# Layer-norm shift terms on GpSimd, a normalisation on ScalarE, and a reordered start in a two-block transformer kernel

## The chip, the core and the metric

The kernel runs on one core of a Trainium2 chip. The core has five engines with queues of their own: TensorE (PE in the profile; PEld is its weight load), VectorE (DVE), ScalarE (ACT), GpSimd (POOL) and SyncE (SP), which here only issues DMAs. The metric is the device time of one execution in microseconds (us), the median of several runs.

## The reference, cut to what matters

The sequence has S = 2048 rows of D = 448; H = 16 heads of 28; Fh = 896.

```
mod = silu(c) @ w_mod                 # sa, ca, ga, sb, cb, gb, each 448
h = layernorm(x) * (1 + ca) + sa
q, k, v = h @ wqkv
phi_q = [softmax(q @ w_phi), softmax(-(q @ w_phi))]   # phi_k likewise
o = (phi_q @ (phi_k.T @ v)) / (phi_q @ sum(phi_k) + 1e-6)   # linear attention
x = x + ga * (o @ wo)
h = layernorm(x) * (1 + cb) + sb
z = gelu(h @ w_in);  z1 = z[:, :Fh];  z2 = layernorm(z[:, Fh:])
g = w_sp @ z2 + b_sp                  # w_sp is 2048 x 2048
x = x + gb * ((z1 * g) @ w_out)
```

## The kernel before, in words

The program is `fast_path`, written with a manual schedule: each engine executes its instructions in the order in which the Python code emits them, and a general path for large weights exists that this input doesn't take. There are NT = 16 tiles of 128 rows. Products accumulate in PSUM, in four single banks (`bank`) and two double banks (`bank2`).

**Setup (lines 541 to 709).** First loads go out on the queues of SP and ScalarE. `silu(c)` is made as a column (`scol`); `colform` multiplies it by slices of w_mod and gives a modulation vector as a column. Scale and shift of the layer norm are folded into the weights: `fold_T` transposes raw k weights on TensorE, `fold_pf` multiplies them by the block-diagonal matrix `BD` of w_phi and by 1 + ca (`ca1`), `fold_sa` and `bias_row` make the bias rows. `l1_stats`, `l1_rstd` and `l1_apply` normalise a tile of x: VectorE takes mean and variance (L603, L604), GpSimd adds epsilon (L608) and raises to the power -0.5 (L609), VectorE forms the shift term `nmr` = -mean * rstd (L611), and the tile is scaled and shifted (L616) and transposed by a DMA on SP (L618).

**Stage 1 (lines 847 to 894)** loops over the tiles: products with Wv and Wk (`k_mm`), two exponentials on ScalarE, the softmax normalisation on VectorE (`k_norm`), accumulation of phi_k.T @ v (`kv_acc`). In the same loop q's weights are folded (`late`), q's products and exponentials are made for four tiles at once (`q_mm`, `q_exp`), and the loads of all later weights are issued (`loads`, `load_wsp`). SP takes its DMAs in order, so that a load stands behind the transposes emitted ahead of it. At the end `KVbd` is built from the accumulator, and `norm_sq` and `norm_max` test the weights' norms for the flag that chooses the path.

**Stage 2 (lines 998 to 1021)** is a software pipeline over j = 0 to 23. Iteration j works on eight different tiles:

```
l2_apply(j-4)   # L608, L609 GpSimd; L611 nmr VectorE; L616 GpSimd; DMA transpose to h2T
num_fin(j-1)    # L917 Sx ScalarE; L919-L926 cr .. t VectorE; L928 GpSimd; DMA to oT
z2_norm(j-7)    # L983 VectorE
wo_mm(j-3)      # L937, L939 TensorE; L940 ScalarE
z2_stats, z2_rstd(j-6)   # L969, L971 VectorE; L977, L978 GpSimd
l2_stats(j-3)   # L603, L604 VectorE
z2_mm(j-5)      # L960 TensorE; L963 Gelu ScalarE
z1(st, fc)      # L990 TensorE, L991 Gelu ScalarE: j 9 to 20, two of 7 chunks (one each 4th j)
num_mm(j)       # L909 TensorE
```

At j = 21 the last seven z1 units run. The order within an iteration is the order on each engine's queue.

**Stage 3 (lines 1031 to 1068)** multiplies w_sp by z2 in 28 groups of 16 matmuls (`g_unit`, L1035), adds b_sp, multiplies by z1, and makes the output product (L1042).

## Time and profile before

| what | value |
|---|---|
| median of 3 runs | 318.06 us (318.04 to 318.09) |
| profiled execution, its own time | 317.58 us |
| its span, first to last instruction | 315.7 us |
| TensorE busy | 266.4 us (84%) |
| VectorE busy | 179.2 us (57%) |
| ScalarE busy | 94.1 us (30%) |
| GpSimd busy | 92.1 us (29%) |

The profiled execution's own time is 1.9 us longer than its span. Busy shares are means over stages with different limits. The first product of stage 1 starts at 20.70 us, the first of stage 2 at 87.72 us, the first of stage 3 at 190.12 us.

### The profile page before, as it was taken

The page shows a single profiled execution, that of the slowest core. Times are in us where ns is not written, and L with a number is a line of the kernel's source. Part 1 is how long each engine was busy: PE and PEld are TensorE (multiplying, and loading weights), DVE is VectorE, ACT ScalarE, POOL GpSimd, SP SyncE. Part 2 cuts the span into 40 slices and gives each one's busy share as a digit, 9 for nine tenths or more (in the row PEclk, how much of TensorE's full clock was granted, in tenths as well). Part 3 has the DMA queues.
Part 4 walks back from the last instruction along what each step waited for, and adds up shares of the span by engine and source line. Part 5 has one row for each costly group of instructions (what it writes and reads, how often), then busy time and mean ns, then how long its engine had stood idle before and what let it go on. Part 6 is the DMA issues. An engine that isn't in the chain of part 4 may idle for free. (4 is left out here: it accounts for less than half of the span.)

```text
span 315.7 us, 4217 instructions
## 1 busy us (share of the span) xinstructions
PE 266.4 (84%) x1500; PEld 132.0 (42%) x1524; DVE 179.2 (57%) x395; ACT 94.1 (30%) x179; POOL 92.1 (29%) x174
## 2 busy tenths in 40 slices
...
GB/s 184 121 144 122 204 227 243 110 103 166 49 17 50 68 53 33 50 52 39 47 52 51 33 203 173 208 220 2 15 29 15 2 29 28 4 16 15 31 0 65
DMA packets 71038, 25.81 MB, mean 82 GB/s; under 512 B 60960, under 2 KB 70880, under 8 KB 71008
## 3 DMA queue, kind: packets, MB, share of 16 engines
...
## 5 line engine op out<-in xcount | busy, mean ns | idle before, releaser
L1035 PE MATMUL g_ps<-f_wsp,f_z2n 128*128 128x512 bf16 x437 | 97.7, 379 | 0.5
L1035 PEld LDWEIGHTS <-f_z2n 128*128 128x128 bf16 x448 | 43.9, 98 | 52.2
L1037 DVE TENSOR_TENSOR gb<-g_ps,f_bsp 128x512 f32<-128x512 f32 x28 | 19.4, 692 | 69.4 <-PE g_ps L1035 67.4
L960 PE MATMUL z_ps<-f_win,h2T 128*128 128x448 bf16 (+1 forms) x128 | 27.1, 354 | 13.6 <-DMA h2T<-f_xpad 13.6
L990 PE MATMUL z_ps<-h2T,f_win 128*128 128x512 bf16 (+1 forms) x106 | 25.6, 379 | 0.3
L928 POOL TENSOR_TENSOR f_opad<-t 128x448 bf16<-128x448 bf16 x16 | 18.4, 1151 | 23.8 <-DVE t L926 19.3
L616 POOL TENSOR_SCALAR f_xpad<-f_x,rstd,nmr 128x448 bf16<-128x448 bf16 x30 | 22.6, 757 | 8.9 <-DVE nmr L611 3.1
L1042 PE MATMUL o_ps<-f_wout,f_z1T 128*128 128x448 bf16 x112 | 23.6, 352 | 1.8 <-DVE ot L1046 1.8
L963 ACT ACTIVATE z2g<-z_ps 128x896 bf16<-128x896 f32 x16 | 14.7, 917 | 30.7 <-PE z_ps L960 26.6
L960 PEld LDWEIGHTS <-h2T 128*128 128x128 bf16 (+1 forms) x128 | 11.2, 97 | 27.1 <-DMA h2T<-f_xpad 17.8
L939 PE MATMUL x_ps<-f_wo,oT 128*128 128x448 bf16 x64 | 17.9, 381 | 3.1 <-DMA oT<-f_opad 3.1
L1038 DVE TENSOR_TENSOR f_z1T<-gb,f_z1T 128x512 bf16<-128x512 f32 x28 | 19.4, 692 | 1.9 <-DVE gb L1037 0.5
L759 ACT ACTIVATE f_Eq<-q_ps 112x1024 bf16<-112x1024 f32 x16 | 16.2, 1024 | 13.2 <-PE q_ps L753 13.1
L753 PE MATMUL q_ps<-f_hT,f_Wq 128*128 128x512 bf16 (+1 forms) x57 | 14.8, 379 | 4.8 <-DVE f_Wq L663 2.4
L731 DVE TENSOR_REDUCE sums<-f_E 128x32 f32<-128x896 bf16 x16 | 17.2, 1072 | 2.4 <-ACT f_E L726 2.4
L969 DVE BATCH_NORM_STATS2 stats<-z2g 128x6 f32<-128x448 bf16 x32 | 18.3, 615 | 0.1
L991 ACT ACTIVATE f_z1T<-z_ps 128x512 bf16<-128x512 f32 x28 | 16.7, 597 | 4.3 <-PE z_ps L990 4.3
L926 DVE TENSOR_TENSOR t<-num,w 128x896 bf16<-128x896 f32 x16 | 17.5, 1091 | 0.6
L720 PE MATMUL v_ps<-f_Wv,f_hT 128*128 128x448 bf16 x64 | 16.2, 379 | 1.0 <-DMA f_hT<-f_xpad 0.9
L990 PEld LDWEIGHTS <-f_win 128*128 128x128 bf16 x112 | 10.9, 97 | 12.8
L1042 PEld LDWEIGHTS <-f_z1T 128*128 128x128 bf16 x112 | 11.0, 98 | 11.8 <-issue 1.0
L909 PE MATMUL num<-f_KVbd,f_Eq 112*128 112x120 bf16 x128 | 10.0, 226 | 6.9 <-ACT z2g L963 3.0
...
## 6 DMA issues: line engine op xcount, KB each, us to landing
...
```

Source lines behind the costliest of these rows:

```text
L616: eng.tensor_scalar(out=xp[:, 0:D], in0=x_sb[:, i, :], scalar1=rstd[:, t:t + 1], scalar2=nmr[:, t:t + 1], op0=ALU.mult, op1=ALU.add)
L731: nc.vector.tensor_reduce(out=sums[:], in_=E[:].rearrange("p s (c f h) -> p (s c) h f", c=4, h=HP), axis=AX.X, op=ALU.add)
L926: nc.vector.tensor_tensor(out=t[:], in0=nv[:, :, :, 0:DH], in1=w[:].unsqueeze(3).to_broadcast([P, 2, H, DH]), op=ALU.mult)
L928: nc.gpsimd.tensor_tensor(out=op_[:, 0:D], in0=t[:, 0].rearrange("p h d -> p (h d)"), in1=t[:, 1].rearrange("p h d -> p (h d)"), op=ALU.add)
L939: nc.tensor.matmul(x1[:, 0:D], lhsT=oT[0:KD[cc], cc, :], rhs=wo_s[0:KD[cc], cc, :], start=False, stop=(cc == KC - 1))
L960: nc.tensor.matmul(z_ps[:, hf, 0:D], lhsT=h2[0:KB[kc], kc, il * P:(il + 1) * P], rhs=win_s[0:KB[kc], kc, FH + hf * D:FH + (hf + 1) * D], s ...
L969: nc.vector.bn_stats(out=stats[:, hf, :], in_=z2gs[i][:, hf, :])
L990: nc.tensor.matmul(z_ps[:], lhsT=win_s[0:KB[kc], kc, fc * P:(fc + 1) * P], rhs=h2[0:KB[kc], kc, :], start=(kc == 0), stop=(kc == KC - 1))
L1035: nc.tensor.matmul(g[:], lhsT=z2n[:, s_, fc * P:(fc + 1) * P], rhs=wsp_tiles[tcn][:, s_, :], start=(s_ == 0), stop=(s_ == NT - 1))
L1037: nc.vector.tensor_tensor(out=gb[:], in0=g[:], in1=bsp[:, tsl], op=ALU.add)
L1038: nc.vector.tensor_tensor(out=z1T[:, fc, tsl], in0=gb[:], in1=z1T[:, fc, tsl], op=ALU.mult)
L1042: nc.tensor.matmul(o_ps, lhsT=z1T[:, fc, t * P:(t + 1) * P], rhs=wout_s[:, fc, :], start=(fc == 0), stop=(fc == FC - 1))
```

## The change

The shift term of a layer norm (`nmr`) is computed by GpSimd, one instruction a tile, in place of VectorE. z2 is normalised by ScalarE (Identity with a scale and a bias operand), a few calls later in the iteration, and its shift term is made by GpSimd. In setup the k weights come on SP's queue, c comes as a row and is transposed by TensorE, `BD` is made by GpSimd, 1 + ca is made before the fold, `fold_T` alternates ScalarE and VectorE for k too, and weight slices and pads are widened to 128 columns. In stage 1 k's product comes ahead of v's; the late steps move two iterations forward; squares of the weights (`norm_sq`) are spread over iterations 4 to 11; the scaling of `win_s` goes from VectorE (iterations 14 and 15) to GpSimd (12 to 15); wsp0's transposes go from iterations 10 to 13 to 13 to 15 and after; w_out's load goes from iteration 6 to the start of stage 2, b_sp's from iteration 7 to the end of stage 2. The last q product is made in two halves in single banks, with the norm products between, ahead of kv_acc(15).

```diff
-    wk_raw = aph.tile([P, KC, D], BF, name="f_wk_raw")
+    wk_raw = aph.tile([P, KC, D + 16], BF, name="f_wk_raw")
...
-        nc.sync.dma_start(out=cT[:], in_=c.rearrange("o (k p) -> p (o k)", p=DC))
+    nc.sync.dma_start(out=c_row[:], in_=c)
     nc.scalar.dma_start(out=wm1[:, :, D:960], in_=wmod_v[:, :, D:960])
     nc.sync.dma_start(out=x_sb[:, 0:2, :], in_=xv[:, 0:2, :])
-    load_rows(nc.scalar, wk_raw[:], A_wqkv[:, D:2 * D])
-    nc.sync.dma_start(out=x_sb[:, 2:4, :], in_=xv[:, 2:4, :])
     nc.scalar.dma_start(out=wm1[:, :, 0:D], in_=wmod_v[:, :, 0:D])
+    load_rows(nc.sync, wk_raw[:, :, 0:D], A_wqkv[:, D:2 * D])
...
+    nc.sync.dma_start(out=x_sb[:, 2:4, :], in_=xv[:, 2:4, :])
     load_rows(nc.sync, Wv[:], A_wqkv[:, 2 * D:3 * D])
...
-        nc.vector.scalar_tensor_tensor(out=nmr[:, 0:n], in0=mv[:, 0:n, 0], scalar=-1.0, in1=rstd[:, 0:n], op0=ALU.mult, op1=ALU.mult)
+        for t in range(n):
+            nc.gpsimd.tensor_scalar(out=nmr[:, t:t + 1], in0=mv[:, t, 0:1], scalar1=rstd[:, t:t + 1], scalar2=-1.0,
+                                    op0=ALU.mult, op1=ALU.mult)
...
-    fold_T(wk_raw, wTk, False)
     l1_rstd(0)
-    l1_apply(0, nc.vector)
-    l1_apply(1, nc.vector)
-    l1_stats(2)
-    l1_stats(3)
-    nc.vector.tensor_tensor(out=BD[:].rearrange("p g (f h) -> p g f h", h=HP),
+    nc.gpsimd.tensor_tensor(out=BD[:].rearrange("p g (f h) -> p g f h", h=HP),
...
     one_plus(colform(wm1, 1), ca1)
+    l1_apply(0, nc.vector)
+    l1_apply(1, nc.vector)
+    fold_T(wk_raw, wTk)
     for m in range(3):
-        fold_pf(wTk, Wk, m, 0)
+        fold_pf(wTk, Wk, m, m % 2)
+    l1_stats(2)
+    l1_stats(3)
+    l1_rstd(1)
     cf = colform(wm1, 0)
     nc.vector.tensor_copy(out=sapad[:, :, 64], in_=cf[:, 0:4])
-    l1_rstd(1)
+    fold_sa(wk_raw, wTk)
     bv = bias_row(sapad, Wv, 0, D)
-    fold_sa(wk_raw, wTk)
+    fold_pf(wTk, Wk, 3, 0)
...
-        elif i == 5:
+        elif i == 13:
             nc.sync.dma_start(out=wmg[:, :, D:2 * D], in_=wmod_v[:, :, 5 * D:6 * D])
-        elif i == 6:
-            nc.sync.dma_start(out=wout_s[:], in_=B_w_out.rearrange("(k p) n -> p k n", p=P))
-        elif i == 7:
-            nc.sync.dma_start(out=bsp[:], in_=B_b_sp.partition_broadcast(P))
...
+        if 4 <= i < 12:
+            norm_sq((i - 4) // 4, (i - 4) % 4)
+        if i >= 12:
+            kk = i - 12
+            nc.gpsimd.tensor_scalar(out=win_s[0:KD[kk], kk, :], in0=win_s[0:KD[kk], kk, :], scalar1=cb1[0:KD[kk], kk:kk + 1],
+                                    scalar2=0.0, op0=ALU.mult, op1=ALU.add)
...
-        if 10 <= i < 14:
-            load_wsp(0, i - 10)
-        if i == 13:
-            norm_sq(0)
+        if i >= 13:
+            load_wsp(0, i - 13)
+    load_wsp(0, 3)
...
+    for u in range(2):
+        q1 = bank("q1_ps")
+        cc = 2 + u
+        for kc in range(KC):
+            nc.tensor.matmul(q1[:], lhsT=Wq[0:KB[kc], kc, cc * CB:cc * CB + P], rhs=hT[0:KB[kc], kc, 3 * 512:4 * 512],
+                             start=(kc == 0), stop=(kc == KC - 1))
+        n_pss.append(norm_mm(u))
+        for s in range(2):
+            nc.scalar.activation(out=Eq[0:CB, cc, s, 3 * 512:4 * 512], in_=q1[0:CB, :], func=ACT.Exp, scale=1.0 - 2.0 * s)
     kv_acc(NT - 1)
...
-    norm_max(0)
-    norm_sq(1)
-    q_mm(7)
-    q_exp(7, 0)
-    q_exp(7, 1)
-    norm_max(1)
+    for u in range(2):
+        nc.vector.tensor_reduce(out=mx[:, u:u + 1], in_=n_pss[u][0:1, 0:D], axis=AX.X, op=ALU.max)
...
-        z2mv[i] = (mv, rstd)
+        nmr = sm.tile([P, 1], F32, tag="z2nm")
+        nc.gpsimd.tensor_scalar(out=nmr[:], in0=mv[:, 0, 0:1], scalar1=rstd[:], scalar2=-1.0, op0=ALU.mult, op1=ALU.mult)
+        z2mv[i] = (nmr, rstd)
...
-        nc.vector.tensor_scalar(out=z2n[:, i, :], in0=z2gs.pop(i)[:].rearrange("p a d -> p (a d)"), scalar1=mv[:, 0, 0:1], scalar2=rstd[:],
-                                op0=ALU.subtract, op1=ALU.mult)
+        nc.scalar.activation(out=z2n[:, i, :], in_=z2gs.pop(i)[:].rearrange("p a d -> p (a d)"), func=ACT.Identity, scale=rstd[:],
+                             bias=nmr[:])
...
+    nc.sync.dma_start(out=wout_s[:], in_=B_w_out.rearrange("(k p) n -> p k n", p=P))
     for j in range(NT + 8):
...
-        if on(j - 7):
-            z2_norm(j - 7)
         if on(j - 3):
             wo_mm(j - 3)
...
             l2_stats(j - 3)
+        if on(j - 7):
+            z2_norm(j - 7)
         if on(j - 5):
             z2_mm(j - 5)
...
+    nc.sync.dma_start(out=bsp[:], in_=B_b_sp.partition_broadcast(P))
```

## Rows read from the trace of the kernel before

**Rows 1.** Stretches: length, busy time and instructions of each engine, PEclk, DMA share, GB/s.
```profile
20.70:87.70 67.00, 60.52 (x428) 32.95 (x433) 51.10 (x103) 43.62 (x74) 23.07 (x33) 1.00 0.70 157
...
119.30:171.60 52.30, 41.62 (x236) 19.76 (x239) 40.47 (x107) 22.89 (x49) 31.73 (x55) 1.00 0.24 46
171.60:190.10 18.50, 16.44 (x77) 7.20 (x77) 10.84 (x26) 10.16 (x16) 10.71 (x21) 1.00 0.57 111
190.10:307.60 117.50, 116.92 (x547) 54.52 (x557) 45.16 (x68) 0.60 (x1) 3.73 (x4) 1.00 0.25 52
```

**Rows 2.** Timeline of VectorE, 128 to 139 us: start, duration, instruction, idle before.
```profile
130.19 0.19 DVE L919 TENSOR_TENSOR cr<-num,Sx 128x32 f32<-128x32 f32 x1
...
132.26 0.50 DVE L983 TENSOR_SCALAR f_z2n<-z2g,z2mv,rstd 128x896 bf16<-128x896 bf16 x1
...
135.90 0.16 DVE L611 SCALAR_TENSOR_TENSOR nmr<-l2mv,rstd 128x1 f32<-128x1 f32 x1 [1.12 <-POOL rstd L609]
```

**Rows 3.** Timeline of TensorE, 128 to 139 us.
```profile
133.59 1.69 PE L960 MATMUL z_ps<-f_win,h2T 128*128 128x448 bf16 x8 [0.86 <-DMA h2T<-f_xpad]
135.12 1.90 PE L990 MATMUL z_ps<-h2T,f_win 128*128 128x512 bf16 x7
136.86 0.58 PE L909 MATMUL num<-f_KVbd,f_Eq 112*128 112x120 bf16 x8
```

**Rows 4.** Timeline of TensorE, 106 to 115 us.
```profile
109.73 0.58 PE L909 MATMUL num<-f_KVbd,f_Eq 112*128 112x120 bf16 x8 [0.97 <-ACT z2g L963]
110.14 0.35 PE L937 MATMUL x_ps<-f_x,f_ident 128*128 128x448 bf16 x1
...
111.29 1.69 PE L960 MATMUL z_ps<-f_win,h2T 128*128 128x448 bf16 x8
113.99 0.58 PE L909 MATMUL num<-f_KVbd,f_Eq 112*128 112x120 bf16 x8 [1.01 <-ACT z2g L963]
```

**Rows 5.** Timeline of GpSimd, 128 to 139 us.
```profile
132.43 1.23 POOL L928 TENSOR_TENSOR f_opad<-t 128x448 bf16<-128x448 bf16 x1 [1.25 <-DVE t L926]
134.16 0.22 POOL L977 TENSOR_SCALAR rstd<-z2mv 128x1 f32<-128x1 f32 x1 [0.51 <-DVE z2mv L971]
...
135.01 0.22 POOL L608 TENSOR_SCALAR rstd<-l2mv 128x1 f32<-128x1 f32 x1
...
136.23 0.75 POOL L616 TENSOR_SCALAR f_xpad<-f_x,rstd,nmr 128x448 bf16<-128x448 bf16 x1 [0.36 <-ACT z2g L963]
```

**Rows 6.** Timeline of GpSimd, 106 to 115 us.
```profile
109.67 1.03 POOL L928 TENSOR_TENSOR f_opad<-t 128x448 bf16<-128x448 bf16 x1 [1.25 <-DVE t L926]
```

**Rows 7.** Groups of ScalarE by line and shape: count, busy us, mean ns, idle.
```profile
L991 ACT ACTIVATE f_z1T<-z_ps 128x512 bf16<-128x512 f32 x28 | 16.7, 597 | 4.3 <-PE z_ps L990 4.3
...
L963 ACT ACTIVATE z2g<-z_ps 128x896 bf16<-128x896 f32 x16 | 14.7, 917 | 30.7 <-PE z_ps L960 26.6 <-DVE stats L969 4.1
...
L940 ACT CAST f_x<-x_ps 128x448 bf16<-128x448 f32 x16 | 8.5, 532 | 16.3 <-PE x_ps L939 16.3
...
L661 ACT ACTIVATE f_Wk<-pf,f_ca 128x448 bf16<-128x448 f32 x3 | 1.7, 632 | 3.0 <-PE pf L658 3.0
...
L963 ACT ACT_TABLE_LOAD x1 | 1.3, 1283 | 0.0
```

**Rows 8.** Timeline of TensorE in setup.
```profile
14.03 1.30 PE L658 MATMUL pf<-f_BD,f_wTk 112*128 112x112 bf16 x12 [2.50 <-DVE f_BD L692]
...
20.70 1.70 PE L720 MATMUL v_ps<-f_Wv,f_hT 128*128 128x448 bf16 x4
```

**Rows 9.** Timeline of TensorE in stage 1.
```profile
39.95 1.48 PE L753 MATMUL q_ps<-f_hT,f_Wq 128*128 128x512 bf16 x6 [2.42 <-DVE f_Wq L663]
...
61.46 0.93 PE L720 MATMUL v_ps<-f_Wv,f_hT 128*128 128x448 bf16 x4 [0.95 <-DMA f_hT<-f_xpad]
```

**Rows 10.** Timeline of VectorE at the end of stage 1.
```profile
82.72 0.63 DVE L883 TENSOR_TENSOR f_KVbd<-kvacc,f_mask 112x464 bf16<-112x464 f32 x1
```

**Rows 11.** Timeline of GpSimd in the second half of stage 1.
```profile
67.30 1.42 POOL L616 TENSOR_SCALAR f_xpad<-f_x,rstd,nmr 128x448 bf16<-128x448 bf16 x2 [0.30 <-DVE nmr L611]
```

More of the change, by code (lines that the diff above doesn't have):

```diff
@@ L535, in fast_path @@
     vring = [aph.tile([P, H, DH + 1], BF, name=f"f_vaug{r}") for r in range(3)]
-    cT = aph.tile([DC, KC], BF, name="f_cT")
+    c_row = aph.tile([1, D], BF, name="f_c_row")
     e = aph.tile([DC, KC], F32, name="f_e")
@@ L539, in fast_path @@
     scb = aph.tile([DC, KC, P], BF, name="f_scb")
-    sapad = aph.tile([P, KC, 65], BF, name="f_sapad")
-    sbpad = aph.tile([P, KC, 65], BF, name="f_sbpad")
+    sapad = aph.tile([P, KC, P], BF, name="f_sapad")
+    sbpad = aph.tile([P, KC, P], BF, name="f_sbpad")
     ca1 = aph.tile([P, KC], F32, name="f_ca1")
@@ L545, in fast_path @@
     wTq = aph.tile([CB, 4, D + 1], BF, name="f_wTq")
-    sq = aph.tile([P, KC, D], BF, name="f_sq")
+    sqs = [aph.tile([P, KC, D], BF, name=f"f_sq{r}") for r in range(2)]
     mx = aph.tile([1, 2], F32, name="f_mx")
@@ L579, in fast_path @@
         nc.gpsimd.memset(xpad[r][:, D:D + 1], 1.0)
+        if r == 1:
+            nc.gpsimd.memset(wk_raw[:, :, D:D + 16], 0.0)
+    nc.gpsimd.memset(wq_raw[:, :, D:D + 16], 0.0)
     nc.gpsimd.memset(Wq[:, :, D:D + 16], 0.0)
@@ L592, in fast_path @@
         nc.vector.tensor_copy(out=KVbd[:, s, :, :, 29], in_=mask[:].unsqueeze(1).to_broadcast([P, 4, HP]))
-    nc.scalar.activation(out=e[:], in_=cT[:], func=ACT.Exp, scale=-1.0)
+    ct_ps = bank_bf("ct_ps")
+    for kk in range(KC):
+        nc.tensor.transpose(ct_ps[0:DC, 2 * kk:2 * kk + 1], c_row[0:1, kk * DC:(kk + 1) * DC], ident[0:1, 0:1])
+    ctv = ct_ps[0:DC, 0:8].rearrange("p (k t) -> p k t", t=2)[:, :, 0]
+    nc.scalar.activation(out=e[:], in_=ctv, func=ACT.Exp, scale=-1.0)
     nc.vector.tensor_scalar(out=e[:], in0=e[:], scalar1=1.0, scalar2=None, op0=ALU.add)
     nc.vector.reciprocal(out=e[:], in_=e[:])
-    nc.vector.tensor_tensor(out=scol[:], in0=e[:], in1=cT[:], op=ALU.mult)
+    nc.vector.tensor_tensor(out=scol[:], in0=e[:], in1=ctv, op=ALU.mult)
     def stats_of(src, mv_t, tagp):
@@ L638, in fold_T @@
             for m in range(KC):
-                nc.tensor.transpose(tps[0:CB, m * P:m * P + KD[m]], wraw[0:KD[m], m, g * CB:(g + 1) * CB],
+                nc.tensor.transpose(tps[:, m * P:m * P + KD[m]], wraw[0:KD[m], m, g * CB:g * CB + P],
                                     ident[0:KD[m], 0:KD[m]])
-            if g % 2 == 0 or not alt:
+            if g % 2 == 0:
                 nc.scalar.copy(out=wT[:, g, 0:D], in_=tps[0:CB, 0:D])
@@ L719, in k_mm @@
         for kc in range(KC):
+            nc.tensor.matmul(k_ps[:, 0:D], lhsT=hT[0:KB[kc], kc, i * P:(i + 1) * P], rhs=Wk[0:KB[kc], kc, :], start=(kc == 0), stop=(kc == KC - 1))
+        for kc in range(KC):
             nc.tensor.matmul(v_ps[:, 0:D], lhsT=hT[0:KB[kc], kc, i * P:(i + 1) * P], rhs=Wv[0:KB[kc], kc, :], start=(kc == 0), stop=(kc == KC - 1))
-        for kc in range(KC):
-            nc.tensor.matmul(k_ps[:, 0:D], lhsT=hT[0:KB[kc], kc, i * P:(i + 1) * P], rhs=Wk[0:KB[kc], kc, :], start=(kc == 0), stop=(kc == KC - 1))
-        nc.scalar.copy(out=vring[i % 3][:, :, 0:DH], in_=v_ps[:, 0:D].rearrange("p (h f) -> p h f", f=DH))
         E = Ering[i % 3]
```

44 lines of the change are left out of this document (17 added, 27 removed).

## The prediction, on record before the changed kernel ran

> **What bounds the kernel now.** I read the stretches first, then one period of stage 2 engine by engine, then the price list, then what TensorE waited for in setup and stage 1. The stretches [rows 1] show three regimes. From 190.1 us on, the last stage keeps TensorE busy 116.9 of 117.5 us: nothing in the change touches its matmuls, so it keeps its length. The stretch from 119.3 to 171.6 us, the loop over j = 9 to 18 of stage 2, has TensorE busy 41.6 of 52.3 us and no other engine fuller, so something passes a wait round. That stretch is nine periods of 52.3 / 9 = 5.81 us.
>
> Inside a period VectorE shows it [rows 2]: its only idle time is 1.12 us ahead of `nmr` (L611), released by GpSimd's power (L609). VectorE produces the variances, GpSimd makes rstd, VectorE waits for it to make the shift term `nmr`, and all VectorE work of the next tile (cr, t, the statistics) stands behind that wait. 1.12 plus VectorE's own work fills 5.8 us. TensorE's wait for h2T (0.86 us, [rows 3]) is the echo: the transpose starts after GpSimd's apply, which stood behind `nmr`.
>
> **Stage 2, part by part.** (1) `nmr` of the second layer norm moves to GpSimd: VectorE loses the 1.12 us wait and the instruction (0.16). (2) z2's normalisation leaves VectorE: 0.50 us [rows 2]. VectorE's period becomes 5.81 - 1.12 - 0.16 - 0.50 = 4.0 us.
>
> ScalarE takes z2's normalisation. The trace has no 128x896 Identity with two pointer operands; a plain 128x896 ScalarE pass is 0.917 us, and 128x448 costs 0.632 with one pointer operand (L661) against 0.532 without (L940), so 0.10 a pointer [rows 7]. Between 0.92 and 1.12 I take 1.12. ScalarE's period: 0.53 (L940) + 1.12 + 0.92 + 2 x 0.60 (two z1 units) = 3.8; with the two 16-column copies of Sx I put it at 4.1.
>
> GpSimd gains two 128x1 tensor_scalar. The same shape, L608, takes 0.22, and I charge 0.30 from start to start. From L608's start to the apply's (L616) pass 1.22 us, 0.36 of them idle, so sum and power take 0.86 [rows 5]. Its period: 0.86 + 0.30 + 0.75 for the layer norm, the add L928, and 0.86 + 0.30 for z2's rstd, which has the same two instructions: 3.07 + L928. L928 took 1.03 us at 109.67, before z2_norm had begun on VectorE [rows 6], and 1.23 in the full period, where it starts 0.17 us after z2_norm [rows 2, 5]. So 4.1 to 4.3; without z2_norm on VectorE I take 4.2.
>
> The Trainium skill, "SBUF — State Buffer", section "SBUF: two separate sides", says the port pair that VectorE and GpSimd share is an exclusive lock for a whole instruction in VectorE's wide modes. By that rule L928 would lose the 0.33 us left of z2_norm, and GpSimd's period would fall by that much, from 4.3 to about 4.0; by the row it falls by 0.20. Both stay under TensorE's, so the total is the same by either; and no run here shows that the other wide VectorE passes do not lock it out in other places.
>
> TensorE's period with two z1 units: z2 to z1 1.53, z1 to num 1.74 [rows 3], num to x1 0.41, x1 to z2 1.15 [rows 4]: 4.83 us. This is the largest of the four, so it becomes the bound. With one z1 unit it is 0.87 less, 3.96, but then another loop holds: num waits for the Gelu of the same iteration (4.26 us from 109.73 to 113.99, with 1.01 us of waiting, [rows 4]). In it z2_norm fits between L940 and the Gelu: x1 to L940's end is about 1.15 + 0.1 + 0.53, plus 1.12 gives 2.9, just when z2's matmuls are done. So 4.3.
>
> j = 9 to 18: six periods with two z1 units 29.0, two with one 8.6, one without num 4.4: 42.0 instead of 52.3, so -10.3 if every hand-off is hidden. GpSimd at 4.2 waits in order for three VectorE results, so I charge 0.17 a period and take -8.8. Bounds: -10.3, and -4.6 (rival A).
>
> Of what ScalarE now waits for: z2_norm waits for GpSimd's shift term of the iteration before; behind it stand the Gelu and the z1 Gelus, and TensorE's num waits for the Gelu. From cr to z2's epsilon (L977) pass 3.97 us [rows 2, 5], 0.50 less without L983; 0.86 + 0.30 more makes the term, and cr begins some 0.5 after x1: ready 5.1 us into its iteration, 0.3 into the next, where z2_norm's turn comes 1.8 in. Slack 1.5 us.
>
> (3) j = 4 to 8 lose the same kind of `nmr` wait, but from j = 6 the Gelu loop already sets 4.26 us. At most four waits (-4.5), at least nothing; I take -1.5, one period and a little of j = 8. (4) The tail, 171.6 to 190.1 us: TensorE busy 16.4 of 18.5 [rows 1]; its waits for h2T shrink, bounds 0 and -2.1, I take -1.5. The last z2_norm on ScalarE comes after the seventh Gelu of z1(3); the first g group needs that tile in its 16th matmul, over 3 us later (eight of 512 columns take 1.74, [rows 3]), and 0.6 + 1.12 fits: nothing. wsp's columns 1 to 3 now go out behind bsp: one more issue on SP, for tiles needed a chunk later: nothing. bsp itself is first needed after the first g group.
>
> **Setup.** TensorE's chain from f_wk_raw to the first k/v product has one long hole: the fold's matmuls wait 2.50 us for BD, which VectorE makes late, behind two more tiles' statistics [rows 8]. BD moves to GpSimd, and its place is ahead of everything that waits there; ca1 is made before the fold too. -2.5. wk_raw moves from ScalarE's queue to SP's behind two x tiles and might land later, so nothing to -3 (the 128-wide weight slices could give some tenths). The transposes of hT(2, 3) and the loads behind them on SP start earlier by about 1 us only.
>
> **Stage 1.** VectorE loses one `nmr` wait (taken as in stage 2, [rows 2]) for each pair of tiles, which shows where it is late: q's first product waits 2.42 us for VectorE's f_Wq, and one k/v product 0.95 us for hT behind the wide loads [rows 9]. Both could go; x tiles 4 to 7, which VectorE's queue needs next, arrive only about 1 us earlier, so I take -2.0 of 3.4. Squares and the four scalings of f_win go to GpSimd, which is busy for 23.1 of these 67 us [rows 1]: hidden. By L616's 0.75 for 448 columns a scaling of 1792 is about 3 us, 12 in all; they can begin when the last apply of the stage is done, and from then (67.30 + 1.42, [rows 11]) to the stage's end are 19 us. If that cover went, z2's first product would wait for it. wout leaves SP right after wsp0 and should land before the first oT; if not, that oT and the first x1 are later: not in the sum, inside the range.
>
> The end of stage 1 is rebuilt: q(7) no longer waits for the one free double bank, but kv_acc(15) comes after it, so that the two KVbd products (0.63 each, [rows 10]) and their corrections are no longer hidden. The loss is at most these, 1.7; the gain at most what was hidden behind, q(7)'s eight matmuls (1.74, as two z1 units, [rows 3]); I take 0, and +0.4 for the two maxima that now stand ahead of the first cr on VectorE.
>
> **Sum.** -2.5 - 2.0 + 0.4 - 1.5 - 8.8 - 1.5 = -15.9. The profiled execution took 317.58 us (span 315.7 and 1.9 around it): 301.7; the median before is 0.5 above that execution, so 302.0. This case alone runs from 297 to 305.
>
> **Rivals.** A. GpSimd sets the pace: its three in-order waits do not overlap its 4.2 us of work and the period is about 5.3. For it: it is within 0.6 us of the bound. Against: VectorE can run ahead by a ring of two. Nine periods 47.7: 306. B. The front gives nothing (wk_raw lands later, VectorE still stuck behind x): 302 + 4.5 = 306.5. C. The wait returns on ScalarE: GpSimd's shift term comes over 1.5 us later than worked out, z2_norm holds the Gelu, num waits; from 2.5 us late the period is 5.8 again: 302 + 8.8 + 1.5 = 312. D, the other side: Identity isn't in the function table loaded for Gelu (the single load took 1.28 us, [rows 7]), and each z2_norm brings two loads. ScalarE's period becomes 4.1 + 2.57 = 6.7 and sets the pace: nine times 0.9 above today's 5.8, j = 7 and 8 and the five tail iterations some 2 us each (estimates), less the front's 5: 317.6 + 8 + 14 - 5 = 335. It decides as soon as one such pair per iteration is there. Against it: L940's plain copies stand between Gelus with one load in all [rows 7].
>
> The Trainium skill, "ScalarE: Activation LUTs", section "Table sets: the hidden batching unit", says that cheap functions, identity among them, are in every set; by it D does not happen, and the trace agrees for copies, with one load in stage 2.
>
> Under 0.2% (0.6 us) this measurement can hardly tell from no change.
>
> **Chances.** Forecast 0.62, A 0.18, B 0.07, C 0.06, D 0.04; 0.03 for something unnamed that eats it all. The range 297 to 308 takes in the forecast, A and B and most of the bounds. Faster 0.93, same 0.02, slower 0.05.
>
> **What would show it.** Right: no VectorE wait for L609's power in stage 2; num to num about 4.9 us in j = 9 to 16 with TensorE's waits for h2T gone; one table load for Gelu; first k/v product near 18 us; q's first wait under 1 us. Wrong: ScalarE's z2_norm released by GpSimd's nmr with TensorE's num behind it; GpSimd without idle time at a period over 5; ACT_TABLE_LOAD beside z2_norm; a first oT that is late.

## The result and the profile after

The changed kernel took 308.56 us (median of 4, 305.93 to 310.02) against 318.07 for the kernel before: a ratio of 0.9686, 95% interval 0.9605 to 0.9766. The forecast was 302.0 with a range of 297 to 308, so the gain came, but it is 9.5 us where 15.9 were worked out. Runs more than 1.5% above the fastest of their kernel are left out of every ratio below but not out of the medians, so where the two differ the ratio counts.

The profiled execution took 309.96 us (span 308.1). Its stretches, cut at the events of [rows 1] (first k product, first numerator product, end of the ninth numerator product, first x1 product of j = 18, first g product), with length, busy time of TensorE, its weight loads, VectorE, ScalarE and GpSimd, granted clock, DMA share and GB/s:

```profile
17.21:88.18 70.97, 61.09 (x429) 32.20 (x433) 51.90 (x88) 43.80 (x78) 34.12 (x49) 0.98 0.66 144
88.18:118.95 30.77, 20.97 (x134) 10.53 (x134) 25.34 (x64) 11.71 (x30) 17.92 (x33) 0.83 0.24 49
118.95:166.25 47.30, 42.43 (x236) 20.28 (x238) 34.25 (x91) 32.81 (x59) 36.40 (x78) 0.96 0.26 54
166.25:182.39 16.14, 16.09 (x78) 7.39 (x78) 5.68 (x14) 13.98 (x20) 9.87 (x23) 1.00 0.61 125
182.39:299.90 117.51, 116.89 (x547) 54.48 (x557) 45.17 (x69) 1.62 (x2) 3.98 (x5) 1.00 0.27 56
```

The columns of lengths give the account. The first numerator product moved from 87.72 to 88.18 us: setup and stage 1 gave -4.5 in the forecast and +0.5 on the chip. The stretch from there to j = 9 went from 31.58 (87.72 to 119.30) to 30.77, -0.8 where -1.1 was forecast. The nine iterations behind it went from 52.30 to 47.30: -5.0 where -8.8 was forecast. (The prediction calls them j = 9 to 18; they are j = 9 to 17, from one x1 product to another, and x1 of tile 15 begins j = 18.) The tail went from 18.50 to 16.14, -2.4 where -1.5 was forecast, and the last stage kept its length. So 5.0 us are missing in front and 3.8 in the loop. This execution is 1.4 us above its kernel's median and the profiled one of the kernel before 0.5 below, so that the stretches show a gain of 7.6 us and not of 9.5; some of what is missing is therefore this execution's own (e7 below, with the same front, has its first numerator product at 86.04).

**Front.** TensorE in setup and stage 1 (start, duration, idle before and its releaser), which answers to [rows 8, 9]:

```profile
17.21 1.70 PE L728 MATMUL k_ps<-f_Wk,f_hT 128*128 128x448 bf16 x4
...
24.64 1.71 PE L647 MATMUL tps<-f_ident,f_wq_raw 128*128 128x128 bf16 x16 [2.70 <-DMA f_wq_raw<-in_A_wqkv_dram]
...
36.51 1.48 PE L761 MATMUL q_ps<-f_hT,f_Wq 128*128 128x512 bf16 x6 [1.19 <-DVE f_Wq L671]
...
43.34 0.93 PE L728 MATMUL k_ps<-f_Wk,f_hT 128*128 128x448 bf16 x4 [2.61 <-DMA f_hT<-f_xpad]
44.12 1.61 PE L730 MATMUL v_ps<-f_Wv,f_hT 128*128 128x448 bf16 x4
...
75.58 0.59 PE L751 MATMUL kvacc<-f_vaug,f_phik 128*128 128x116 bf16 x8 [1.79 <-DVE f_phik L743]
```

The first product is 3.5 us earlier than in [rows 8], more than forecast, and the wait for BD is gone. It is given back in three places, where the kernel before waits 0.21 us or not at all: 2.70 us for `f_wq_raw`, 2.61 for hT of tile 6, 1.79 for `f_phik`. SP's queue shows why the first is there:

```profile
9.21 10.23 SPq L626 DMA_TRANSPOSE f_hT<-f_xpad  x4
19.50 0.57 SPq L787 DMA_DIRECT2D f_x<-in_A_x_dram  x1
20.13 0.50 SPq L556 DMA_DIRECT2D f_wq_raw<-in_A_wqkv_dram  x1
...
34.23 0.58 SPq L796 DMA_DIRECT2D f_wm<-in_w_mod_dram  x1
36.70 1.19 SPq L626 DMA_TRANSPOSE f_hT<-f_xpad  x1
```

The loads of x tiles 4 to 7 and of wq stand in SP's order behind the transposes of tiles 2 and 3, and are issued at 19.50 and 20.13 us; in the kernel before it was 19.41 and 20.05. TensorE started 3.5 us earlier, and the loads that it needs next were issued when they always were; VectorE stood idle for the same x tiles for 5.99 us, until 23.43 (2.09, until 23.31, in the kernel before). The transpose of tile 6 went out at 36.70 behind the 840 KB of `f_wm`, and the product that reads it began 6.6 us later; the median from issue to landing of these transposes is 2.4.

The third wait is VectorE's, held by GpSimd. The scalings of `f_win` on GpSimd, and the product of the same time on VectorE:

```profile
69.84 7.31 POOL L834 TENSOR_SCALAR f_win<-f_win,f_cb 128x1792 bf16<-128x1792 bf16 x4
```
```profile
66.89 0.63 DVE L743 TENSOR_TENSOR f_phik<-f_E,r 128x896 bf16<-128x896 bf16 x1
...
70.64 4.89 DVE L743 TENSOR_TENSOR f_phik<-f_E,r 128x896 bf16<-128x896 bf16 x1
```

The same instruction takes 0.63 us without a scaling beside it and 4.89 beside four of them.

**End of stage 1.** VectorE, behind the products of [rows 10]:

```profile
88.75 1.13 DVE L896 TENSOR_REDUCE f_mx<-n_ps 1x1 f32<-1x448 f32 x2
...
90.80 0.19 DVE L924 TENSOR_TENSOR cr<-num,Sx 128x32 f32<-128x32 f32 x1 [0.56 <-ACT Sx L922]
```

**Stage 2.** VectorE, 128 to 139 us, for [rows 2]; GpSimd in one iteration of its own pace, for [rows 5, 6]; ScalarE's groups, for [rows 7]:

```profile
132.74 0.19 DVE L924 TENSOR_TENSOR cr<-num,Sx 128x32 f32<-128x32 f32 x1 [0.64 <-ACT Sx L922]
```
```profile
115.71 0.22 POOL L982 TENSOR_SCALAR rstd<-z2mv 128x1 f32<-128x1 f32 x1
...
116.68 0.30 POOL L985 TENSOR_SCALAR nmr<-z2mv,rstd 128x1 f32<-128x1 f32 x1
117.06 0.22 POOL L614 TENSOR_SCALAR rstd<-l2mv 128x1 f32<-128x1 f32 x1
...
118.03 0.26 POOL L618 TENSOR_SCALAR nmr<-l2mv,rstd 128x1 f32<-128x1 f32 x1
118.39 0.71 POOL L624 TENSOR_SCALAR f_xpad<-f_x,rstd,nmr 128x448 bf16<-128x448 bf16 x1
119.07 1.03 POOL L933 TENSOR_TENSOR f_opad<-t 128x448 bf16<-128x448 bf16 x1
120.19 0.22 POOL L982 TENSOR_SCALAR rstd<-z2mv 128x1 f32<-128x1 f32 x1
```
```profile
L990 ACT ACTIVATE f_z2n<-z2g,nmr,rstd 128x896 bf16<-128x896 bf16 x16 | 18.1, 1132 | 1.7 <-POOL nmr L985 1.7
...
L968 ACT ACT_TABLE_LOAD x1 | 1.3, 1283 | 0.0
```

VectorE waits no more for GpSimd's power; the wait left is for Sx, ScalarE's copy from TensorE's numerator. ScalarE's new pass costs 1.13 us (1.12 taken), with one table load. GpSimd runs without idle time at 4.48 us (115.71 to 120.19), where 4.2 was forecast. From start to start, each pair of sum and power takes 0.97 (115.71 to 116.68, 117.06 to 118.03), not 0.86, and the shift terms 0.38 and 0.36, not 0.30; L933 takes 1.12, as was taken. TensorE, for [rows 3, 4]:

```profile
117.00 1.69 PE L965 MATMUL z_ps<-f_win,h2T 128*128 128x448 bf16 x8 [1.22 <-DMA h2T<-f_xpad]
...
122.00 2.51 PE L965 MATMUL z_ps<-f_win,h2T 128*128 128x448 bf16 x8 [1.83 <-DMA h2T<-f_xpad]
124.73 2.37 PE L997 MATMUL z_ps<-h2T,f_win 128*128 128x512 bf16 x7 [0.22 <-issue]
...
131.77 0.58 PE L914 MATMUL num<-f_KVbd,f_Eq 112*128 112x120 bf16 x8
...
136.60 0.58 PE L914 MATMUL num<-f_KVbd,f_Eq 112*128 112x120 bf16 x8
...
140.57 0.58 PE L914 MATMUL num<-f_KVbd,f_Eq 112*128 112x120 bf16 x8
...
143.15 1.69 PE L965 MATMUL z_ps<-f_win,h2T 128*128 128x448 bf16 x8 [0.94 <-DMA h2T<-f_xpad]
```

Two numerators with two z1 units between them are 4.83 us apart (131.77, 136.60), the forecast to the hundredth. But the waits for h2T are not gone. Those at j = 8 and 9 (1.22 and 1.83; the expectation of e12 below calls them j = 7 and 8) follow GpSimd's pace, and behind the second z2 takes 2.51 us instead of 1.69, at a granted clock of 0.79 over this iteration, part of it at 1.2 instead of 2.4 GHz:

```profile
118.95:127.00 8.05, 6.00 (x26) 2.52 (x24) 4.89 (x14) 4.02 (x7) 6.87 (x16) 0.79 0.31 67
```

From num of j = 8 (118.53) to num of j = 9 (126.94) pass 8.41 us. The wait at 143.15, and one of 1.36 at 162.99, have another cause (GpSimd, then SP):

```profile
138.96 0.71 POOL L624 TENSOR_SCALAR f_xpad<-f_x,rstd,nmr 128x448 bf16<-128x448 bf16 x1
```
```profile
140.80 1.19 SPq L626 DMA_TRANSPOSE h2T<-f_xpad  x1
```

GpSimd's apply of tile 8 was done at 139.67, yet its transpose was issued at 140.80, when z1's last products of block 0 (139.70 to 140.73) had ended. A block is four tiles; tile 8 is the first of block 2, and h2T has two buffers, so that it takes the one that z1 of block 0 was reading. The wait at 162.99 is that of tile 12, the first of block 3. (The expectation of e7 below calls them tiles 12 and 16.)

### The profile page after: what moved, and what is told of

The parts are those of the page before. It is cut to its first block, busy times and chain, and to the rows that moved or that the text cites. A ratio compares the mean times of both kernels' runs of the same rounds, so it can differ in the third digit from the quotient of the medians.

```text
span 308.1 us, 4290 instructions
## 1 busy us (share of the span) xinstructions
PE 267.0 (87%) x1505; PEld 130.7 (42%) x1528; DVE 174.4 (57%) x353; ACT 107.8 (35%) x194; POOL 111.3 (36%) x229
## 4 chain that ended last, share of the span: by engine, by line
PE 63%; DVE 10%; DMA 9%; issue 8%; POOL 6%; ACT 1%; SPq 1%; POOLq 0%; DVEq 0%; ACTq 0%
PE g_ps L1044 31%; PE z_ps L997 7%; PE o_ps L1051 7%; PE z_ps L965 6%; DMA h2T<-f_xpad 3%; DMA f_hT<-f_xpad 2%; DMA f_wk_raw<-in_A_wqkv_dram 2%; PE x_ps L944 2%; PE k_ps L728 2%; PE q_ps L761 2%; PE v_ps L730 2%; DVE f_phik L743 1%; DVE stats L609 1%; POOL f_xpad L624 1%; DVE sums L739 1%
## 5 line engine op out<-in xcount | busy, mean ns | idle before, releaser
L965 PE MATMUL z_ps<-f_win,h2T 128*128 128x448 bf16 (+1 forms) x128 | 27.9, 361 | 6.7 <-DMA h2T<-f_xpad 6.7
L997 PE MATMUL z_ps<-h2T,f_win 128*128 128x512 bf16 (+1 forms) x106 | 26.3, 386 | 0.5 <-issue 0.2
L933 POOL TENSOR_TENSOR f_opad<-t 128x448 bf16<-128x448 bf16 x16 | 16.5, 1030 | 23.9 <-issue 16.0
L624 POOL TENSOR_SCALAR f_xpad<-f_x,rstd,nmr 128x448 bf16<-128x448 bf16 x30 | 21.3, 711 | 1.7
L767 ACT ACTIVATE f_Eq<-q_ps 112x1024 bf16<-112x1024 f32 x14 | 14.3, 1031 | 13.7 <-PE q_ps L761 13.7
L990 ACT ACTIVATE f_z2n<-z2g,nmr,rstd 128x896 bf16<-128x896 bf16 x16 | 18.1, 1132 | 1.7 <-POOL nmr L985 1.7
L728 PE MATMUL k_ps<-f_Wk,f_hT 128*128 128x448 bf16 x64 | 15.6, 368 | 2.6 <-DMA f_hT<-f_xpad 2.6
L743 DVE TENSOR_TENSOR f_phik<-f_E,r 128x896 bf16<-128x896 bf16 x16 | 17.0, 1062 | 1.3
```

The costliest lines, as they stand in the source:

```text
L624: eng.tensor_scalar(out=xp[:, 0:D], in0=x_sb[:, i, :], scalar1=rstd[:, t:t + 1], scalar2=nmr[:, t:t + 1], op0=ALU.mult, op1=ALU.add)
L728: nc.tensor.matmul(k_ps[:, 0:D], lhsT=hT[0:KB[kc], kc, i * P:(i + 1) * P], rhs=Wk[0:KB[kc], kc, :], start=(kc == 0), stop=(kc == KC - 1))
L743: nc.vector.tensor_tensor(out=pring[i % 3][:, 0:2 * D].rearrange("p (a f h) -> p a f h", a=8, h=HP), in0=E[:].rearrange("p s (c f h) -> p ...
L965: nc.tensor.matmul(z_ps[:, hf, 0:D], lhsT=h2[0:KB[kc], kc, il * P:(il + 1) * P], rhs=win_s[0:KB[kc], kc, FH + hf * D:FH + (hf + 1) * D], s ...
L997: nc.tensor.matmul(z_ps[:], lhsT=win_s[0:KB[kc], kc, fc * P:(fc + 1) * P], rhs=h2[0:KB[kc], kc, :], start=(kc == 0), stop=(kc == KC - 1))
```

## Experiments

**Each half alone.** Stage 2's part on the kernel before (nmr of the second layer norm on GpSimd, z2 normalised on ScalarE; front untouched), and the changed kernel with stage 2's norms put back:

```
e1:  before  + nmr of l2 on GpSimd + z2_norm on ScalarE behind l2_stats
e2:  after   - nmr of l2 on GpSimd - z2_norm on ScalarE
```

> The kernel before with only the stage 2 part of the change: the second layer norm's shift term and z2's on GpSimd, z2 normalised by ScalarE and called after l2_stats. Setup, stage 1 and all loads as before. Theory (the gain of the changed kernel is all made in stage 2; its front gives nothing back): 9 to 10 us under before, 308 to 309 us; GpSimd without idle time for j = 5 to 9 at a period of 4.4 to 4.5 us, and TensorE's num to num at 4.83 us with two z1 units. Rival (the front gives its 4 us and stage 2 only the rest): 313 to 314 us.

> The changed kernel with stage 2's layer norms as before: the second layer norm's shift term on VectorE, z2 normalised by VectorE at its old place. Setup, stage 1, its loads and the first layer norm as changed. Theory (the earlier start runs into loads and VectorE waits and is lost by the end of stage 1): 318 to 320 us, the first num product at 88 to 89 us. Rival (the front gives 4 us as predicted and the profiled run hid it): 314 us, num at 84 us.

Measured: e1 309.16 us, ratio 0.9705 (0.9679 to 0.9731); e2 317.91 us, ratio 1.0004 (0.9971 to 1.0037). Stage 2 is the whole of the gain, and the front as changed is worth nothing (e2's first numerator product is at 88.45). Both theories hold, to 0.2 us of their ranges.

**What the front lost.** The loads of x tiles 4 to 7 and of wq put ahead of the applies of tiles 2 and 3 (e4), and the scalings of f_win put back on VectorE (e3):

```diff
e4
+    loads(-1)
     l1_apply(2, nc.gpsimd)
     l1_apply(3, nc.gpsimd)
...
-    loads(-1)
e3
-            nc.gpsimd.tensor_scalar(out=win_s[0:KD[kk], kk, :], in0=win_s[0:KD[kk], kk, :], scalar1=cb1[0:KD[kk], kk:kk + 1],
-                                    scalar2=0.0, op0=ALU.mult, op1=ALU.add)
+            nc.vector.tensor_scalar(out=win_s[0:KD[kk], kk, :], in0=win_s[0:KD[kk], kk, :], scalar1=cb1[0:KD[kk], kk:kk + 1],
+                                    scalar2=None, op0=ALU.mult)
```

> The changed kernel with the four scalings of f_win in iterations 12 to 15 on VectorE, one an iteration, in place of GpSimd. Theory (GpSimd's 7.3 us of scalings shut VectorE's f_phik product out for 4.9 us, and TensorE's kv product waits 1.8 us for it): that f_phik falls to 0.6 us, TensorE's wait goes, the first num product comes 1.5 to 2.5 us earlier than in the changed kernel: 306 to 307 us. Rival (VectorE was late there anyway, and 0.65 us more an iteration takes the place of the lock): within 0.5 us of the changed kernel's 308.6.

> The changed kernel with the loads of x tiles 4 to 7 and of f_wq_raw issued on SP ahead of the transposes of tiles 2 and 3. Theory (TensorE waits 2.7 us for f_wq_raw because SP holds its issue behind two transposes that wait for GpSimd's apply): the wait falls under 0.5 us and q's first product comes some 2 us earlier; but the hT transpose of tile 6 still lands behind f_wm2's 840 KB, so the later wait for hT grows and half of it is lost again: 307 to 308 us, the first num product at most 1 us earlier. Rival (the issue was the only bound and nothing stands behind it): num 2.7 us earlier, 306 us.

Measured: e3 308.06 us, ratio 0.9603 (0.9566 to 0.964). Its four times go from 304.98 to 310.22, the changed kernel's from 305.93 to 310.02, so theory and rival are not told apart. e4 305.01 us, ratio 0.9586 (0.9545 to 0.9628). In e4 SP issues the loads at 11.69 and 12.32 us, and the wait for `f_wq_raw` is gone (SP's queue, then TensorE):

```profile
11.69 0.57 SPq L694 DMA_DIRECT2D f_x<-in_A_x_dram  x1
12.32 0.50 SPq L556 DMA_DIRECT2D f_wq_raw<-in_A_wqkv_dram  x1
```
```profile
21.10 1.68 PE L647 MATMUL tps<-f_ident,f_wq_raw 128*128 128x128 bf16 x16
...
39.63 1.68 PE L748 MATMUL k_ps<-f_Wk,f_hT 128*128 128x448 bf16 x4 [3.32 <-DMA f_hT<-f_xpad]
...
83.41 0.37 PE L914 MATMUL num<-f_KVbd,f_Eq 112*128 112x120 bf16 x4 [0.24 <-DVE f_KVbd L893]
```

Its first numerator product stands at 83.41 us, 4.8 before the changed kernel's and 2.6 before the 86.04 of e7. The wait for hT of tile 6 has grown to 3.32, since TensorE now arrives there earlier, but half of the gain was not lost to it: the theory misses, and the rival (2.7 us earlier, 306 us) is nearer. Both edits together:

> The changed kernel with the two edits together that each gave back time in stage 1: the loads of x tiles 4 to 7 and of wq ahead of the applies of tiles 2 and 3, and the f_win scalings on VectorE. Theory (the late loads cost the first half of stage 1, the scalings that hold VectorE its last third, and the two add): first numerator product at about 81 us, 302 to 304 us. Rival (both remove the same slack): the first numerator product stays near 83.4 and the time near 305.

Measured: 304.81 us, ratio 0.9559 (0.9531 to 0.9587), first numerator product at 80.51. The 16 f_phik products take 11.0 us, as before the change (10.8; 17.0 in the changed kernel, 13.8 in e4), and the wait ahead of kvacc is gone:

```profile
L763 DVE TENSOR_TENSOR f_phik<-f_E,r 128x896 bf16<-128x896 bf16 x16 | 11.0, 685 | 1.3
```

That the hold of VectorE is gone is plain; what it is worth in time is not, because e8's interval overlaps e4's: the numerator is where the theory has it, the time where the rival has it.

**Stage 2's two moves apart**, each alone on the kernel before. In e5 only the layer norm's shift term is on GpSimd; in e6 only z2's normalisation is on ScalarE, its shift term made as in the change.

```diff
e5 (l2 only)
-        nc.vector.scalar_tensor_tensor(out=nmr[:, 0:n], in0=mv[:, 0:n, 0], scalar=-1.0, in1=rstd[:, 0:n], op0=ALU.mult, op1=ALU.mult)
+            nc.gpsimd.tensor_scalar(out=nmr[:, 0:1], in0=mv[:, 0, 0:1], scalar1=rstd[:, 0:1], scalar2=-1.0, op0=ALU.mult, op1=ALU.mult)
e6 (z2_norm, called behind l2_stats)
-        nc.vector.tensor_scalar(out=z2n[:, i, :], in0=z2gs.pop(i)[:].rearrange("p a d -> p (a d)"), scalar1=mv[:, 0, 0:1], scalar2=rstd[:],
-                                op0=ALU.subtract, op1=ALU.mult)
+        nc.scalar.activation(out=z2n[:, i, :], in_=z2gs.pop(i)[:].rearrange("p a d -> p (a d)"), func=ACT.Identity, scale=rstd[:],
+                             bias=nmr[:])
```

> The kernel before with only the second layer norm's shift term moved from VectorE to GpSimd; z2 is still normalised on VectorE. Theory (the 1.12 us wait passed round between VectorE and GpSimd set the period of 5.8 us, and its removal is most of stage 2's gain): the period of j = 9 to 16 falls to about 5.0 us and the time to 310 to 312 us. Rival (both parts are needed, since VectorE's z2 norm keeps GpSimd's additions slow and late): 313 to 316 us.

> The kernel before with only z2's normalisation moved to ScalarE, with its shift term on GpSimd; the second layer norm's shift term stays on VectorE. Theory (VectorE's wait for the power stays and grows by what VectorE's work loses): 315 to 319 us, VectorE's wait ahead of the second layer norm's shift term 1.4 to 1.8 us instead of 1.12. Rival (0.50 us of VectorE work per period is worth its length wherever it stands): 312 to 314 us.

Measured: e5 ratio 0.9695 (0.9658 to 0.9731), 309.0 to 315.8 us with a median of 313.27; e6 320.72 us, ratio 1.0055 (1.0035 to 1.0074). By the ratio the shift term alone gives what both moves give together (e1, 0.9705); by e5's median, which lies in its rival's range, it doesn't. Its times are too far apart to settle it here; e11 below, on a repaired kernel, agrees with the ratio. Moving z2's normalisation alone makes the kernel 0.5% slower, a little past the theory's 319, and the rival of e6 is out. VectorE in e6 keeps its wait and has it longer, 1.67 us instead of 1.12, as the theory had it; GpSimd shows the z2 term made ahead of the layer norm's sum and power that VectorE waits for:

```profile
155.50 0.16 DVE L611 SCALAR_TENSOR_TENSOR nmr<-l2mv,rstd 128x1 f32<-128x1 f32 x1 [1.67 <-POOL rstd L609]
```
```profile
154.26 0.26 POOL L980 TENSOR_SCALAR nmr<-z2mv,rstd 128x1 f32<-128x1 f32 x1
154.61 0.22 POOL L608 TENSOR_SCALAR rstd<-l2mv 128x1 f32<-128x1 f32 x1
```

The 0.50 us off VectorE turned into waiting, and with the extra GpSimd instruction (0.35 us from start to start) the nine periods take 54.31 us instead of 52.28. In e5 numerators with two z1 units between them are 4.83 us apart, as in the changed kernel (132.20 and 137.03).

**The h2T ring** of the changed kernel with a third buffer:

```diff
-            h2Ts[st] = sm.tile([P, KC, 512], BF, name="h2T", tag="h2T", bufs=2)
+            h2Ts[st] = sm.tile([P, KC, 512], BF, name="h2T", tag="h2T", bufs=3)
```

> The changed kernel with three h2T buffers instead of two. Theory (tiles 12 and 16, the first of a block of four, write their transpose only when z1 of the block before the last has read the old buffer, and the two waits of 0.94 and 1.36 us are paid by TensorE): 1 to 2.5 us faster than the changed kernel, 306 to 307.5 us. Rival (GpSimd's late apply is behind these waits too): no difference.

Measured: 307.74 us, ratio 0.9654 (0.9616 to 0.9691). The wait at tile 8 is gone, and its transpose goes out at 135.35, before z1's last products of block 0 (135.37 to 136.40; TensorE, then SP):

```profile
137.80 1.69 PE L965 MATMUL z_ps<-f_win,h2T 128*128 128x448 bf16 x8
...
154.14 2.58 PE L965 MATMUL z_ps<-f_win,h2T 128*128 128x448 bf16 x8 [1.77 <-DMA h2T<-f_xpad]
```
```profile
135.35 1.19 SPq L626 DMA_TRANSPOSE h2T<-f_xpad  x1
```

The mechanism is as the theory says, at tiles 8 and 12; alone it is worth under 1 us by the medians, too little to tell by the interval. In this trace the wait at tile 11 (154.14) is 1.77 us, against 0.29 in the changed kernel's, with z2 at 2.58 us behind it. That is not the ring's doing: e4, with two buffers, has 1.77 there too. What makes this wait differ was not settled.

**Repairs added up.** e9 is e8 with the ring of three; e10 also loads wm2 at tile 3 instead of 2 and the halves of f_win at tiles 5 and 7 instead of 3 and 4; e11 is e10 with z2 normalised on VectorE; e12 is e10 with z1 begun at j = 8.

```diff
e10
-        elif i == 2:
+        elif i == 3:
             nc.sync.dma_start(out=wm2[:], in_=wmod_v[:, :, 3 * D:3 * D + 960])
-        elif i == 3:
+        elif i == 5:
             load_rows(nc.sync, win_s[:, :, 0:FH], B_w_in[:, 0:FH])
-        elif i == 4:
+        elif i == 7:
             load_rows(nc.sync, win_s[:, :, FH:2 * FH], B_w_in[:, FH:2 * FH])
e12
-        if j >= 9 and j < 9 + 12:
-            for fc in range(*z1_split[(j - 9) % 4]):
-                z1((j - 9) // 4, fc)
-        elif j == 21:
+        if j >= 8 and j < 8 + 12:
+            for fc in range(*z1_split[(j - 8) % 4]):
+                z1((j - 8) // 4, fc)
+        elif j == 20:
```

> The changed kernel with the early loads, the f_win scalings on VectorE and three h2T buffers. Theory (the three remove separate waits: two in stage 1, one per block of four tiles in stage 2): num-to-num 4.83 us at j = 13 instead of 5.84 and 302.5 to 304.5 us. Rival (what the ring gives in the loop is waited for again before the last stage): the first g product no earlier after the first numerator product than 93.5 us, and 304.5 to 305.5 us.

> As the run of three edits, and the wide loads of stage 1 spread out: wm2 at tile 3 instead of 2, the two halves of f_win at tiles 5 and 7 instead of 3 and 4. Theory (the transposes of hT for tiles 4 to 7 stand behind these loads in the DMA engines, the 2.2 to 3.3 us wait of a k product at 39 us): that wait falls under 1 us, the first numerator product comes 1 to 2 us earlier, 301 to 303 us. Rival (the transpose is late for another reason, or the later loads delay the f_win fold): no difference to the run of three edits.

> As the run of four edits, but z2 normalised on VectorE as in the kernel before (the second layer norm's shift term stays on GpSimd). Theory (once the shift term is off VectorE, TensorE with two z1 units sets the period at 4.83 us wherever z2 is normalised): within 1 us of the run of four edits. Rival (the 0.50 us on VectorE and the slower GpSimd addition beside it bring waits back): 3 us slower or more.

> As the run of four edits, with z1 begun one iteration earlier (j = 8 instead of 9), so that TensorE has z1 products to do while GpSimd's period of 4.45 us holds z2's. Theory (the waits for h2T at j = 7 and 8 cost 1.2 to 1.8 us each and the clock falls after them): 1 to 3 us faster than the run of four edits. Rival (the z1 products only move and the wait returns at the end of the loop): no difference.

Measured: e9 300.86 us, 0.9413 (0.9379 to 0.9446); e10 298.21 us, 0.9361 (0.9332 to 0.9389); e11 297.56 us, 0.9336 (0.9312 to 0.936); e12 301.21 us, 0.9455 (0.9415 to 0.9496). e9 did better than either theory: the ring, worth under 1 us alone, is worth some 4 on top of e8 (304.81 to 300.86 by the medians), and e9's profile shows where: the nine iterations take 43.32 us instead of e8's 46.94, without the waits at tiles 8 and 12. Why it is so much more than in e7 stays open. In e10 the wait falls as its theory says, for hT of tile 6 from 2.87 (in e9) to 0.37, and the time comes out lower than the theory's 301 to 303. Its windows and its TensorE rows:

```profile
17.10:78.01 60.91, 59.26 (x435) 31.83 (x434) 49.14 (x93) 43.59 (x78) 27.32 (x45) 1.00 0.66 148
...
109.90:152.39 42.49, 41.20 (x245) 19.98 (x243) 33.51 (x87) 32.74 (x59) 34.67 (x76) 1.00 0.32 60
152.39:168.52 16.13, 16.13 (x79) 7.38 (x77) 5.67 (x14) 13.98 (x20) 10.34 (x23) 1.00 0.61 123
```
```profile
40.46 0.93 PE L748 MATMUL k_ps<-f_Wk,f_hT 128*128 128x448 bf16 x4 [0.37 <-DMA f_hT<-f_xpad]
...
78.01 0.37 PE L914 MATMUL num<-f_KVbd,f_Eq 112*128 112x120 bf16 x4 [0.24 <-DVE f_KVbd L893]
```

Stage 1 is 60.91 us long instead of 70.97, and j = 9 to 17 takes 42.49 at full clock, where the forecast had 42.0 if every hand-off is hidden. Part of that is a shift: the iteration at the lower clock is now j = 8 (num to num 5.90 us instead of 4.37), ahead of the cut. From num of j = 7 to x1 of j = 18 pass 57.58 us in the kernel before, 52.09 in the changed one and 48.77 in e10. e10 and e11 beat both kernels, by 20.5 us on the kernel before (298.21 against 318.67 beside it), and they don't differ from each other by their intervals: where z2 is normalised does not matter here. z1 earlier brings nothing, and why e12 is slower than e10 stays open.

**Whose is the front's gain?** e13 puts these repairs on the front of the kernel before, with stage 2 and its ring as in e10; f_win is scaled on VectorE there already. e14 puts them on the changed front with stage 2's norms as before and two h2T buffers.

```diff
e13, on the kernel before with stage 2's two moves
+    loads(-1)
     l1_apply(2, nc.gpsimd)
     l1_apply(3, nc.gpsimd)
...
-        elif i == 2:
+        elif i == 3:
             nc.sync.dma_start(out=wm2[:], in_=wmod_v[:, :, 3 * D:3 * D + 960])
```

The two halves of f_win follow at tiles 5 and 7 here too, and wmg's second half, wout and bsp at tiles 8, 9 and 10 instead of 5, 6 and 7.

> The front of the kernel before (setup, stage 1 and its end unchanged), with the loads of x tiles 4 to 7 and of wq ahead of the applies of tiles 2 and 3, the wide loads spread out as in the run of four edits, stage 2 as changed, and three h2T buffers. Theory (the changed front is worth its setup, 3.5 us at the first product, and about 2 us of VectorE's waits in stage 1, once the loads come in time): 303 to 305 us against 298.2 for the run of four edits, first numerator product at 83 to 85 us. Rival (the repairs are the whole gain and the front's order is worth nothing): 298 to 300 us, first numerator product near 79.

> The changed front with the early loads, the wide loads spread out and the f_win scalings on VectorE, stage 2's two norms as in the kernel before. Theory (the front's repaired gain of 9 to 10 us adds to stage 2 and does not depend on it): 308 to 310 us against 317.9 for the front alone. Rival (part of it is lost to a stage 2 that starts earlier, on loads that come later): 311 to 314 us.

Measured: e13 308.79 us, 0.9703 (0.9661 to 0.9745), first numerator product only at 91.05; e14 311.52 us, 0.9766 (0.9733 to 0.9798), first numerator product at 78.48. On the old front the repairs give nothing at all (e1, without them and without the third buffer, had 0.9705), so that theory and rival both miss. The front itself comes 2.2 us later than e1's (first numerator product at 88.89 there), and stage 2, with its third buffer, is 2.9 us shorter (90.01 against 92.93 to the first g product). TensorE's first product is at 20.63 us, and its waits are those of [rows 9], q's for `f_Wq` and a v product's for hT:

```profile
39.79 2.00 PE L780 MATMUL q_ps<-f_hT,f_Wq 128*128 128x512 bf16 x6 [2.41 <-DVE f_Wq L666]
...
63.24 0.93 PE L747 MATMUL v_ps<-f_Wv,f_hT 128*128 128x448 bf16 x4 [1.75 <-DMA f_hT<-f_xpad]
```

So the changed front is worth 10.6 us (308.79 to 298.21) once its loads come in time, and the early loads are worth nothing without it (the kernel before waits only 0.21 us for `f_wq_raw`): each was hidden by the other. Which part of the front makes the 10.6 is not separated: e13 lacks the new setup, k's product ahead of v's, the first layer norm's shift term on GpSimd, the earlier late steps and the rebuilt end, and it still loads w_out and b_sp in stage 1. In e14 the rival's 311 to 314 holds: from first numerator to first g product stage 2 took 104.7 us (78.48 to 183.2) where the kernel before took 102.4 [rows 1], 2.3 of the front's 9.2 lost again, most of it from num of j = 8 to num of j = 9, which takes 8.02 us where the kernel before takes 6.37, at a granted clock of 0.78 (111.58 to 119.20).

## Why the prediction was wrong, step by step

**The wait in stage 2: right.** VectorE's wait for the power was the circle that set 5.81 us, and without it TensorE sets 4.83 with two z1 units, as worked out. e5 and e6 show that the shift term's move alone does it. For e5 this rests on the ratio. The 0.50 us counted for z2's normalisation was a term of VectorE's period only, and VectorE is not the bound either way (e11).

**Table and ScalarE: right.** Rivals C and D did not come. The Trainium skill, "ScalarE: Activation LUTs", section "Table sets: the hidden batching unit", says identity is in every set, and the trace agrees: 16 passes in stage 2, one load.

**j = 9 to 17 ("9 to 18"), -8.8: mis-sized, -5.0.** Two terms were missing. The ring of two for h2T was not looked at: with a shorter period the first tile of a block catches up with z1 of the block two before (0.94 and 1.36 us, at tiles 8 and 12). And the first iteration began late and at a lower clock, behind h2T waits that GpSimd's pace brought: 8.41 us where the profiles of e4 and e7 have 6.2. GpSimd's 4.48 instead of 4.2 comes from the two pairs of sum and power, priced at 0.86 and taking 0.97, and the two shift terms, priced at 0.30 and costing 0.37. With the third buffer and the front repaired, the stretch is 42.49 (with the lower clock just ahead of it): the step's arithmetic of TensorE was right, its hand-offs were not. That 47.30 is near rival A's 47.7 is chance, since the periods with two z1 units are 4.83 and not 5.3.

**Setup, -2.5: the term was right and the sum wrong.** The first product came 3.5 us earlier. But this was added to the time as if stage 1 would start earlier as a whole; the prediction itself says that the loads behind the transposes on SP start only about 1 us earlier, and then takes nothing off setup's gain for that. They started 0.1 us later, and TensorE waited 2.70 for them. This is the step that failed most: e4, which moves these loads only, is 3.5 us faster than the changed kernel by the medians (308.56 to 305.01; the intervals overlap a little), with its first numerator product 4.8 us earlier.

**Stage 1, -2.0: wrong.** From the first product of the stage to the first of tile 15 it takes 60.5 us (17.21 to 77.74) instead of 55.9 (20.70 to 76.63), +4.6: the three waits above come to 7.1, and others that shrank or went give a part of it back. q's wait did shrink from 2.42 to 1.19, but the transpose of tile 6, stuck in the DMA engines behind wide loads, cost 2.61 and a stretch at a lower clock (v at 44.12 took 1.61 us, 0.92 at full clock); e10 removes it. **The scalings of f_win: "hidden" was wrong in kind.** They took 7.3 us, less than the 12 charged, and GpSimd had the time; what was not asked is whom they hold up on VectorE. The lock that the prediction quoted for L928 was not weighed here, where TensorE waited 1.79 us behind it; what that is worth in the total is not shown (e3, e8). The squares were on GpSimd already; the change only moves them in time.

**End of stage 1 and the maxima, 0 and +0.4: mis-sized.** From the first product of tile 15 to the first numerator product it is 10.4 us instead of 11.1, -0.7 for the 0 that was taken. The two maxima take 1.13 us (88.75) and the flag follows at 90.1; ScalarE's Sx waits for it. The first cr begins 2.6 us after the first numerator product (88.18 to 90.80), in the kernel before 1.1 (87.72 to 88.80): +1.5. **j = 4 to 8, -1.5: the right way, and more**, -2.4 from num of j = 3 to num of j = 8 (22.57 to 20.20 us). **Tail: right in kind**, -2.4 against -1.5, and past the bound of -2.1: with every h2T wait gone it is 16.14, and TensorE's own work in it is 16.1 and not 16.4. (By its own sum the forecast is 302.2, not 302.0.)

Rival B (front gives nothing, 306.5) was the case that came, at a chance of 0.07, together with a loop 3.8 us short of its sum; its reason, VectorE stuck behind x, came too (5.99 us), but k's weights came only 0.1 us later (first transpose at 8.05 instead of 7.92). Repaired, the front gives more than the 4.5 us forecast: e10's first numerator product is 9.7 us ahead of the kernel before's.
